# Three hand-written lists of order, written anew, in a retention and soft mixture-of-experts attention kernel

## The chip, the cores and the metric

The kernel runs on one core of a Trainium2 chip. The metric is the device time of one execution in microseconds. Its engines here: TensorE (PE; its weight loads are PEld), VectorE (DVE), ScalarE (ACT), GpSimd (POOL), and SyncE (SP), which issues all loads and stores.

## The reference

Eight sequences of 576 tokens go through causal retention with 8 heads of 64, and then through four attention experts of which a gate takes two for each token.

```python
scores = scale * np.matmul(q, k.transpose(0, 1, 3, 2))     # retention, all heads
Dmat = np.where(rel >= 0, gamma ** rel, 0.0)
x = np.matmul(scores * Dmat, v)                            # then heads side by side: (8, 576, 512)
logits = x @ w_gate                                        # 4 experts, best 2 of them
w = softmax of the two best logits
for e in range(4):
    qe, ke, ve = x @ wq[e], x @ wk[e], x @ wv[e]           # 64 wide
    a = softmax(scale * qe @ ke.T, causal)
    out += (weight of e, where e is among the two) * (a @ ve @ wo[e])
```

## The kernel before, in words

The tokens are cut into 36 tiles of 128, two chunks of 64 each; nine tiles are a pair of sequences. Eight of the nine hold neighbouring chunks of one sequence, the ninth (n % 9 == 8) holds the last chunk of both. Three tiles make a group; there are 12 groups. A group passes three stages, one step apart:

- retention, tile by tile: loads lx and lk (queries and keys, keys and values), dc (decay of the values), qm, qa, qp (scores of the chunk, their copy, the causal cut), tm, tv (state of the chunk, added to the running state), om, oa (product with the state of earlier chunks, "old"), wm, wv (product with the chunk's own scores, added), sc (scaling), xh, xl (split into a rounded part and a rest).
- projections of the group before: vm, va, vv (expert values and gate logits), g.0 to g.4 (the gate; g.1 is an exponent on ScalarE, the others are VectorE), km, ka and hm, ha (expert keys and queries, two halves each).
- attention of the group before that, by units: s (scores), r (their limit, on VectorE, which reads PSUM), e (exponent), n (factor), ma or mv (norm on ScalarE or VectorE), tt (transposes through TensorE), ca or cv (their copies out of PSUM on ScalarE or VectorE), ym (product with the values), ya, yp (copy and split).
- one step later still: pm (output projection, four blocks of 128 columns), pa (copy and store).

A unit is a tile, or one of the two halves of a ninth tile; so every third group has four units and the others three. In a step j the retention tokens with number i mean tile 3j + i, the projections belong to group j - 1, the units to group j - 2 and the outputs to group j - 3; where that group or unit does not exist, the token does nothing. So the first step has no pm, and s.3 exists in steps 4, 7 and 10 only. The second digit of a token such as tt.21 is the chunk of blocks within the unit, of r, e, ma, mv the expert.

The order is written by hand as three strings of such tokens: HEAD (groups 0 and 1 of the pipeline), STEP (played for j = 2 to 11) and TAIL (the drain; `@13` sets j for the tokens that follow). PE, DVE, ACT and POOL run their instructions exactly in the order in which the tokens name them; SP is not among these engines, and its loads and stores are placed by the framework. `:v` puts a decay, scaling or rest on VectorE, which is on POOL otherwise.

```python
ORDERED = {mybir.EngineType.PE, mybir.EngineType.DVE, mybir.EngineType.Activation, mybir.EngineType.Pool}
...
pool = ctx.enter_context(tc.tile_pool(name="ps", bufs=8, space=bass.MemoryType.PSUM))
ctx.enter_context(tc.manual_schedule(engines=ORDERED))
...
play(HEAD)
for j in range(2, NG):
    play(STEP, j)
play(TAIL, NG)
```

TensorE's array is used in three shapes. qk (L197), st (L170), old (L223), own (L243) and the scores ss (L419, and L427 for halves of a ninth tile) run as 64x64 quarters. The projections pj (L316) and pv (L335), the output po (L565) and the transposes pt (L498) use the full array. The values product ys (L532, L536, L539) uses 128x64 halves. All PSUM tiles come from one pool of eight banks: qk, st, old, own take two, a score unit two or four, every other block one.

Before the lists start, the kernel runs small warming matmuls (L117) and issues the loads of tiles 0 to 3, tables and three of the four weights; fw.o fetches the fourth, wh and wl split a weight into its rounded part and rest, tb fills a table.

## Time and profile before

| | us |
|---|---|
| median of 3 runs (lowest, highest) | 445.7 (445.47, 446.39) |
| the profiled execution's own time | 445.0 |
| its span, first to last instruction | 443.1 |
| TensorE busy | 427.4 (96%) |
| VectorE, ScalarE, POOL busy | 302.4, 275.9, 205.3 |
| mean granted TensorE clock | 0.985 |

The profiled execution's time is 1.9 us above its span, and 0.7 us below the median of the runs. Matmuls are pipelined, so a busy TensorE is not one at its peak: the cost of a block is read from its start to the start of the next. A timeline's row gives start, length, engine, line, operation, output and inputs with their shape, and in brackets the idle time ahead and what ended it.

### The profile page before, as it was taken

Reading aid. Unit: us, or ns where it says so; the run is one execution under the profiler, and the core shown is the slowest. Engines: PE = TensorE matmul, PEld = TensorE weight load, DVE = VectorE, ACT = ScalarE, POOL = GpSimd, SP = SyncE. Lnnn points to the kernel's source line nnn. Section 1 sums busy time; section 2 is a strip of 40 time slices with the busy share of each in tenths; the row PEclk is TensorE's granted clock in tenths of the full one; section 3 lists DMA queues with packets and bytes.
Section 4 is the critical chain, followed back from the end, with each engine's and each line's share of the span. In section 5 each row is a group of like instructions: output and inputs, shape, how many; then the busy total and the mean of one; then the engine's idle time right before and its main releaser. Section 6 shows DMA issues by size and latency. Waiting matters only on the chain.

```text
span 443.1 us, 18830 instructions
## 1 busy us (share of the span) xinstructions
PE 427.4 (96%) x7916; PEld 387.3 (87%) x7916; DVE 302.4 (68%) x1095; ACT 275.9 (62%) x818; POOL 205.3 (46%) x260
## 2 busy tenths in 40 slices
PE   8499899999999999999999999999999999999996
PEld 4489789899879999899988999899988999988796
DVE  1656976877787548668787657687688566567761
ACT  2546585673775566665667477476476658457882
POOL 5516664653744555555644375475365174210300
PEclk9779899999999999999999999999999999999999
DMA  7944641261261144243343046054143001001112
GB/s 267 407 174 155 212 168 47 98 231 36 103 220 40 54 176 135 93 154 115 98 152 115 1 144 218 21 170 172 34 155 128 1 4 72 1 2 38 37 72 72
DMA packets 18899, 50.90 MB, mean 115 GB/s; under 512 B 2304, under 2 KB 9088, under 8 KB 18816
## 3 DMA queue, kind: packets, MB, share of 16 engines
q1 hardware_dynamic: 18816, 49.71, 32.3%
q8 instruction: 63, 1.03, 1.0%
q14 instruction: 20, 0.16, 0.1%
HBM read 40.26 MB, written 9.44 MB: 112 GB/s over the span
## 4 chain that ended last, share of the span: by engine, by line
PE 86%; issue 3%; ACT 2%; DVE 2%; POOL 2%; DMA 2%; SPq 1%; DVEq 0%; POOLq 0%; ACTq 0%
PE pj L316 22%; PE pv L335 11%; PE po L565 11%; PE pt L498 8%; PE ss L419 7%; PE ys L532 7%; PE qk L197 4%; PE own L243 3%; PE old L223 3%; PE st L170 3%; PE ys L539 2%; DMA vk<-vkf 2%; PE ss L427 2%; PE ys L536 2%; POOL p L210 1%
## 5 line engine op out<-in xcount | busy, mean ns | idle before, releaser
L456 ACT ACTIVATE p<-p,nm 128x128 f32<-128x128 f32 (+8 forms) x144 | 79.5, 559 | 6.4 <-DVE nm L443 5.2
L280 POOL TENSOR_TENSOR xl<-x,xh 128x512 fp32r<-128x512 f32 x31 | 41.8, 1349 | 76.9 <-ACT xh L275 76.8
L443 DVE CUSTOM_DVE_ANT_0 p<-ss,mask 128x320 f32<-128x320 f32 (+7 forms) x128 | 51.6, 454 | 16.3 <-PE ss L419 16.1
L210 POOL TENSOR_SCALAR_AFFINE_SELECT p<-p 64x512 f32<-64x512 f32 x72 | 48.9, 679 | 25.5 <-ACT p L204 19.8
L555 POOL CAST yh<-y 128x256 fp32r<-128x256 f32 (+1 forms) x36 | 13.7, 380 | 92.0 <-ACT y L543 92.0
L482 DVE TENSOR_SCALAR p<-p,sm 128x64 f32<-128x64 f32 (+8 forms) x116 | 46.2, 448 | 0.9
L511 DVE COPY pth<-pt 128x512 f32<-128x512 f32 (+2 forms) x56 | 32.5, 624 | 20.9 <-PE pt L498 20.4
L498 PE MATMUL pt<-con,p 128*128 128x128 f32 x360 | 44.4, 273 | 0.1
L263 POOL TENSOR_TENSOR x<-x,gi 128x512 f32<-128x512 f32 x28 | 36.6, 1307 | 16.1 <-DVE x L253 12.5
L498 PEld LDWEIGHTS pt<-con,p 128*128 128x128 f32 x360 | 41.1, 141 | 1.4 <-DVE pth L511 0.4
L480 ACT ACTIVATE p<-p,sm 128x512 f32<-128x512 f32 (+7 forms) x60 | 31.3, 547 | 14.9 <-DVE sm L466 14.7
L532 PE MATMUL ys<-pth,vn 128*64 128x128 f32 (+1 forms) x640 | 39.2, 254 | 0.0
L419 PE MATMUL ss<-k,q 64*64 64x512 f32 (+7 forms) x512 | 37.0, 405 | 0.0
L157 POOL TENSOR_TENSOR vk<-vk,con 128x512 f32<-128x512 f32 x32 | 34.4, 1075 | 0.5 <-DMA vk<-vkf 0.4
L570 ACT ACTIVATE ot<-po 128x384 f32<-128x384 f32 x48 | 22.4, 486 | 19.0 <-PE po L565 18.8
L323 ACT ACTIVATE k<-pj 128x384 f32<-128x384 f32 x24 | 11.8, 491 | 33.7 <-PE pj L316 33.5
L204 ACT ACTIVATE p<-qk 128x256 f32<-128x256 f32 x72 | 23.5, 381 | 14.0 <-PE qk L197 13.5
L532 PEld LDWEIGHTS ys<-pth,vn 128*64 128x64 f32 x640 | 29.0, 138 | 1.4 <-issue 0.9
L253 DVE TENSOR_TENSOR x<-x,own 128x256 f32<-128x256 f32 (+1 forms) x72 | 25.4, 385 | 5.5 <-ACT x L232 4.3
L243 PEld LDWEIGHTS own<-p,vk 64*64 64x64 f32 x1152 | 24.7, 141 | 5.1 <-issue 4.5
L232 ACT ACTIVATE x<-old 128x256 f32<-128x256 f32 (+1 forms) x72 | 22.0, 361 | 11.4 <-PE old L223 11.0
L464 DVE TENSOR_SCALAR sm<-sm 128x4 f32<-128x4 f32 (+1 forms) x40 | 14.8, 371 | 19.6 <-ACT p L456 19.0
(95 smaller groups left out, 1088.2 us busy)
## 6 DMA issues: line engine op xcount, KB each, us to landing
x<-xf SPq DMA_DIRECT2D x36, 512.0 KB, 3.9
...
rg<-wraw SPq DMA_DIRECT2D x1, 8.0 KB, 7.2
```

The lines of the kernel that those rows point to most:

```text
L210: gp.affine_select(w, w, pattern=[[0, 8], [1, 64]], base=0, channel_multiplier=-1, compare_op=OP.is_ge, fill=0.0)
L243: mm(ps[r][HALF[u], g, i], vk[HALF[r], s, 0, 2 * g + u], p[HALF[r], g, s, u], start=True, stop=True)
L280: e.tensor_sub(xl, x32, f(xh))
L316: mm(ps, ww[:, kc, p * 128:(p + 1) * 128], xx[:, kc], start=(i == 0), stop=(i == 11))
L335: mm(ps, xx[:, kc, l0:l0 + 128], ww[:, kc], start=(i == 0), stop=(i == 11))
L419: mm(ps[e][HALF[p]], q[p][HALF[z], l0 + 64 * s:l0 + 64 * s + 64], k[p][HALF[z], kb:kb + ws[e]], start=True, stop=True)
L443: v.tensor_tensor_reduce(p32[:, e, :ws[e]], ps[e], mask[:, 576 - ws[e]:], -1.0, BIG, OP.add, OP.min, nm[:, e:e + 1])
L456: act(p32[:, e, :ws[e]], p32[:, e, :ws[e]], AF.Exp, bias=nm[:, b:b + 1], scale=-1.0, accum_out=sm[:, 0, e:e + 1])
L482: v.tensor_scalar(o, i, rs[:, e:e + 1], None, op0=OP.mult)
L498: nc.tensor.transpose(pt[:, z], src, ident)
L532: mm(py[HALF[z], p], VN[n0 + j][:, e * D:(e + 1) * D], src, start=(j == 0), stop=False)
L565: mm(ps, ww[:, p, d * 128:(d + 1) * 128], yy[:, p], start=(i == 0), stop=(i == 5))
```

## The change

All three lists are replaced; nothing else is touched. Every list still names the same work, so each kernel runs the same blocks of TensorE with the same shapes. What differs:

- STEP begins with qm.1 ahead of om.0. pm.3 comes ahead of vm.2 and pm.2 behind wm.2, where both stood between qm.3 and om.2; qm.3 and om.2 are neighbours now. s.3 comes behind pm.2. The transposes between the projections are placed in fewer runs.
- Scalings sc.1 and sc.2 of STEP go from POOL to VectorE. 22 more norms go to ScalarE, and 10 more transposes' copies to VectorE, over the whole kernel.
- At the end of STEP, g.0 and g.1 come ahead of ca.21, ym.3 ahead of ym.2, and lk.6 is the last token.
- HEAD: dc.0 and dc.2 go to POOL, dc.1 and dc.4 to VectorE, sc.3 and xl.3 to POOL; wm.2 comes ahead of vm.0, tm.3 ahead of both k projections, wl.v ahead of tv.1, and the loads fw.o, lx, lk stand in other places.
- TAIL: hm and km, two output blocks and the last score units change places, with the copies and norms that go with them.

```diff
--- before.py
+++ after.py
@@ -44,38 +44,39 @@
 
 
 HEAD = """
-dc.0:v qm.0 qa.0 qp.0 tm.0 tv.0 dc.1 qm.1 qa.1 qp.1 tb.1 om.0 oa.0 wm.0 wv.0 qm.2 sc.0:v tm.1 wh.v xh.0 wm.1 qa.2
-qp.2 dc.2:v tv.1 om.1 oa.1 tm.2 xl.0 wl.v lk.4 wv.1 tb.2 sc.1:v xh.1 xl.1:v tv.2 @1 vm.0 va.0 @0 wh.k om.2 oa.2 wm.2
-@1 vv.0 @0 wv.2 lx.4 @1 vm.1 va.1 @0 sc.2:v qm.3 dc.3 lk.5 qa.3 wl.k qm.4 qp.3 xh.2 xl.2:v @1 vv.1 @0 wh.q fw.o @1
-km.0 ka.0 @0 tm.3 qa.4 @1 km.1 @0 lx.5 @1 ka.1 @0 tv.3 wl.q qp.4 om.3 oa.3 wm.3 lk.6 dc.4 tb.3 wv.3 dc.5 sc.3:v qm.5
-qa.5 qp.5 xh.3 tm.4 @1 hm.1 @0 tv.4 om.4 oa.4 wm.4 xl.3:v tb.4 @1 ha.1 @0 lx.6 tm.5 @1 vm.2 @0 wv.4 dc.6:v tv.5 @1
-va.2 @0 sc.4 @1 vv.2 hm.0 @0 xh.4 @1 g.0 g.1 @0 qm.6 @1 g.2 @0 xl.4:v lk.8 @1 g.3 @0 lx.7 qa.6 om.5 @1 g.4 @0 oa.5
-qp.6 lk.7 wm.5 wv.5 dc.7:v wh.o @1 ha.0 @0 tm.6 tv.6 sc.5 xh.5 wl.o xl.5:v lk.9 lx.8
+qm.0 dc.0 qa.0 tm.0 fw.o tv.0 qm.1 qa.1 qp.0 qp.1 tb.1 om.0 oa.0 wm.0 dc.1:v wv.0 sc.0:v qm.2 wh.v tm.1 wm.1 qa.2
+xh.0 wl.v qp.2 dc.2 tv.1 om.1 tb.2 tm.2 oa.1 xl.0 wv.1 sc.1:v xh.1 xl.1:v wm.2 @1 vm.0 @0 lx.4 @1 va.0 @0 tv.2 om.2
+oa.2 wv.2 dc.3 @1 vv.0 @0 wh.k @1 vm.1 va.1 @0 sc.2:v lk.4 qm.3 qa.3 wl.k qm.4 qp.3 xh.2 tm.3 xl.2:v qa.4 tb.3
+dc.4:v @1 vv.1 @0 tv.3 lx.5 wh.q @1 km.1 km.0 @0 qp.4 wl.q @1 ka.1 @0 om.3 lk.5 oa.3 @1 ka.0 @0 wm.3 wv.3 dc.5 tm.4
+qm.5 lx.6 qa.5 sc.3 xh.3 qp.5 @1 hm.1 @0 wm.4 tv.4 @1 ha.1 @0 lk.6 om.4 lk.8 tb.4 oa.4 xl.3 tm.5 @1 vm.2 @0 dc.6:v
+wv.4 @1 va.2 @0 tv.5 sc.4 @1 vv.2 hm.0 @0 lx.7 xh.4 @1 g.0 g.1 @0 qm.6 xl.4:v @1 g.2 @0 qa.6 @1 g.3 @0 om.5 qp.6
+lk.7 oa.5 @1 g.4 @0 wm.5 wv.5 lk.9 dc.7:v wh.o @1 ha.0 @0 tm.6 tv.6 sc.5 lx.8 wl.o xh.5 xl.5:v
 """
 
 STEP = """
-dc.2 om.0 qm.1 qa.1 qp.1 s.0 r.00 r.01 oa.0 r.02 r.03 wm.0 wv.0 tm.1 tv.1 sc.0 e.00 e.01 e.02 vm.0 va.0 e.03 n.0
-vv.0 ma.02 xh.0 mv.00 xl.0 mv.01 mv.03 lx.3 vm.1 va.1 vv.1 pm.0 pa.0 pm.1 pa.1 qm.2 dc.3 s.1 r.10 lk.4 om.1 qa.2
-oa.1 r.11 tm.2 r.12 e.11 r.13 wm.1 tv.2 qp.2 vm.2 e.10 e.12 lx.4 wv.1 lk.5 e.13 qm.3 n.1 mv.11 pm.3 pa.3 qa.3 pm.2
-e.32 va.2 om.2 oa.2 vv.2 pa.2 sc.1 mv.12 ma.10 xh.1 xl.1 qp.3 s.2 r.21 r.32 r.20 wm.2 wv.2 tm.3 e.21 r.22 r.23 e.20
-tv.3 s.3 km.0 e.22 e.23 sc.2 r.31 mv.33 r.30 r.33 hm.0 n.2 mv.21 tt.03 ka.0 tt.01 mv.32 e.30 mv.20 ma.13 e.31 n.3
-ma.31 dc.4 ma.30 hm.1 tt.00 ma.23 xh.2 mv.22 ca.23 xl.2 cv.00 ha.1 tt.02 lk.6 tt.10 tt.11 km.1 cv.10 cv.03 ha.0 ka.1
-cv.01 lx.5 cv.02 cv.11 tt.12 tt.20 e.33 ca.20 tt.21 tt.30 ca.12 tt.13 cv.13 tt.22 ca.22 tt.32 ca.21 g.0 cv.30 tt.31
-ym.0 ca.32 ya.0 yp.0 ym.1 tt.23 ca.31 g.1 ya.1 cv.33 yp.1 ym.2 ya.2 ym.3 g.2 tt.33 ya.3 yp.2 yp.3 g.3 g.4
+dc.2 qm.1 qa.1 qp.1 om.0 oa.0 s.0 r.00 r.01 wm.0 e.00 r.02 wv.0 tm.1 e.01 lk.4 sc.0 e.02 r.03 vm.0 tv.1 va.0 e.03
+n.0 cv.23 mv.01 ma.02 xh.0 vm.1 mv.00 pm.0 mv.03 pa.0 pm.1 xl.0 vv.0 lx.3 va.1 qm.2 dc.3 vv.1 pa.1 qa.2 s.1 r.10
+om.1 r.11 oa.1 r.12 r.13 tm.2 e.11 qp.2 tv.2 lx.4 wm.1 wv.1 lk.5 pm.3 e.12 vm.2 e.10 pa.3 e.13 n.1 qm.3 qa.3 va.2
+vv.2 sc.1:v om.2 oa.2 xh.1 ma.12 xl.1 s.2 e.32 r.22 ma.10 qp.3 tm.3 r.32 ma.11 r.21 r.20 r.23 wm.2 wv.2 e.21 pm.2
+pa.2 e.20 tv.3 s.3 r.30 r.31 e.23 sc.2:v e.22 hm.0 n.2 e.31 mv.20 ma.13 ma.21 dc.4 ma.32 e.30 n.3 mv.31 km.0 tt.01
+ma.30 mv.22 tt.10 ka.0 tt.00 cv.00 cv.01 mv.23 tt.03 r.33 xh.2 tt.11 cv.10 ca.03 ha.0 lx.5 tt.02 km.1 tt.12 ka.1
+hm.1 ha.1 cv.02 tt.20 cv.12 ma.33 ca.20 tt.32 tt.22 cv.11 tt.30 tt.31 cv.22 xl.2 tt.21 tt.13 ca.32 tt.23 cv.30 ym.0
+g.0 cv.13 g.1 cv.33 ca.21 ya.0 yp.0 ca.31 ym.1 tt.33 ym.3 ya.1 yp.1 ya.3 g.2 yp.3 ym.2 g.3 e.33 ya.2 yp.2 g.4 lk.6
 """
 
 TAIL = """
-s.0 r.00 r.01 r.02 r.03 e.00 e.01 e.02 e.03 n.0 mv.01 ma.02 s.1 r.10 hm.0 ha.0 r.11 e.10 mv.03 r.12 km.1 km.0 ka.0
-e.11 e.12 r.13 e.13 n.1 mv.11 mv.10 ma.13 hm.1 ka.1 ha.1 ma.12 s.2 r.20 r.23 vm.0 r.21 r.22 e.20 tt.11 e.21 e.22
-va.0 vv.0 e.23 ma.00 n.2 mv.20 mv.23 vm.1 va.1 @13 s.0 @12 vv.1 ma.21 ma.22 @13 r.00 @12 vm.2 @13 r.02 r.03 @12 va.2
-vv.2 g.0 g.1 @13 r.01 @12 g.2 ca.11 g.3 pm.0 g.4 pa.0 pm.1 pa.1 tt.10 tt.02 tt.12 tt.00 ca.10 ca.12 tt.21 ca.21
-tt.13 ca.02 @13 e.00 @12 tt.01 tt.03 tt.20 cv.20 ca.01 tt.22 ca.13 ca.00 ca.23 @13 s.1 @12 ca.03 @13 r.10 r.13 @12
-cv.22 @13 r.12 e.01 r.11 e.02 e.03 n.0 mv.01 e.12 ma.02 mv.03 mv.00 @12 pm.2 pa.2 pm.3 pa.3 tt.23 ym.0 ya.0 yp.0 @13
-e.11 @12 ym.2 ya.2 yp.2 @13 tt.00 cv.00 e.10 r.22 tt.01 cv.01 tt.02 cv.02 tt.03 cv.03 e.13 e.32 @12 ym.1 ya.1 yp.1
-@13 n.1 ma.10 ma.22 ma.11 s.3 r.30 s.2 r.20 ma.12 r.21 r.31 r.32 e.20 e.21 r.33 pm.2 pa.2 e.22 e.23 n.2 pm.1 mv.13
-e.30 pa.1 mv.20 mv.21 e.31 ma.23 pm.0 pa.0 tt.11 ma.32 tt.10 e.33 n.3 ma.31 mv.30 pm.3 tt.33 pa.3 tt.13 tt.12 cv.10
-cv.13 tt.20 cv.20 mv.33 tt.21 ca.11 ca.12 ca.21 tt.22 tt.30 ca.30 tt.31 tt.32 cv.33 ca.22 cv.23 cv.32 ca.31 ym.0
-ym.1 yl.1 ym.2 ym.3 yl.0 yl.2 yl.3 @14 pm.0 pa.0 pm.2 @13 tt.23 @14 pm.1 pa.1 pa.2 pm.3 pa.3 @13 r.23
+s.0 r.00 r.01 r.02 r.03 e.00 e.01 e.02 e.03 n.0 mv.02 s.1 r.10 r.11 e.10 hm.0 r.12 ha.0 e.12 e.11 km.0 km.1 ka.0
+r.13 e.13 n.1 s.2 ma.11 tt.11 hm.1 mv.12 ma.13 ka.1 ha.1 r.20 r.21 vm.0 r.22 e.20 mv.01 r.23 e.21 e.22 va.0 vv.0
+e.23 ma.00 mv.10 n.2 mv.20 vm.1 @13 s.0 @12 va.1 mv.23 ma.21 vv.1 @13 r.02 @12 mv.22 ma.03 @13 r.00 @12 vm.2 va.2
+vv.2 @13 r.03 @12 g.0 g.1 @13 r.01 @12 g.2 cv.11 pm.1 tt.10 g.3 pm.0 g.4 pa.0 tt.21 pa.1 ca.10 tt.02 cv.12 tt.00
+ca.02 tt.12 ca.21 tt.01 tt.03 tt.20 tt.13 ca.00 cv.20 ca.01 @13 e.00 @12 tt.23 tt.22 @13 e.02 @12 cv.23 @13 s.1 r.13
+@12 cv.22 @13 r.12 e.01 r.11 r.10 e.03 n.0 @12 pm.2 ca.13 ca.03 @13 e.12 ma.02 @12 pa.2 @13 ma.03 @12 pm.3 @13 mv.01
+@12 ym.0 ya.0 @13 mv.00 @12 yp.0 @13 e.11 @12 ym.2 ya.2 yp.2 @13 tt.00 tt.03 cv.00 e.10 r.22 tt.01 tt.02 cv.01 cv.02
+ca.03 e.13 @12 ym.1 pa.3 @13 e.32 @12 ya.1 yp.1 @13 n.1 ma.10 ma.22 s.2 r.20 ma.12 r.21 s.3 e.22 ma.11 r.31 e.20
+e.21 r.33 r.30 ma.13 pm.2 pa.2 e.23 e.31 r.32 e.30 pm.0 n.2 pm.1 mv.23 tt.11 pa.1 ma.21 tt.10 cv.10 mv.33 e.33 n.3
+mv.20 pa.0 ma.31 tt.13 tt.12 mv.30 pm.3 tt.21 tt.33 mv.32 cv.13 pa.3 cv.11 tt.20 r.23 ca.20 cv.12 tt.22 tt.30 cv.30
+cv.21 tt.31 cv.22 tt.32 cv.23 ca.32 ym.0 ym.1 ca.31 cv.33 yl.1 ym.2 ym.3 yl.0 yl.2 yl.3 @14 pm.0 pa.0 pm.3 pa.3 pm.2
+@13 tt.23 @14 pm.1 pa.1 pa.2
 """
 
 
```

## The prediction

> **What bounds the kernel now.** I read the page first (busy shares, chain that ended last), then the windows by stage, then TensorE's own timeline, where the gap from one block's start to the next's is what that block costs.
>
> ```profile
> PE 427.4 (96%) x7916; PEld 387.3 (87%) x7916; DVE 302.4 (68%) x1095; ACT 275.9 (62%) x818; POOL 205.3 (46%) x260
> ...
> PE 86%; issue 3%; ACT 2%; DVE 2%; POOL 2%; DMA 2%; SPq 1%; DVEq 0%; POOLq 0%; ACTq 0%
> ```
>
> ```profile
> core 0: us, PE busy (x) PEld busy (x) DVE busy (x) ACT busy (x) POOL busy (x), PEclk, DMA share, GB/s
> ...
> 47.70:50.20 2.50, 0.40 (x28) 0.27 (x19) 2.44 (x8) 1.29 (x2) 1.46 (x3) 1.00 0.73 226
> 50.20:57.00 6.80, 6.78 (x152) 6.66 (x152) 5.77 (x20) 3.81 (x15) 5.90 (x5) 0.75 0.68 230
> ...
> 216.60:256.00 39.40, 39.40 (x756) 35.42 (x751) 28.86 (x104) 25.39 (x71) 19.56 (x27) 1.00 0.31 103
> 390.00:443.10 53.10, 49.27 (x537) 43.51 (x535) 29.35 (x124) 36.32 (x104) 3.33 (x6) 1.00 0.13 46
> ```
>
> TensorE carries 86% of the chain, and a middle step has it busy for all of 39.40 us at a granted clock of 1.00. A list can save time there in two ways only: less TensorE time lost at the joints between blocks, or fewer waits that busy time hides. VectorE has 28.86 of 39.40 us (73%) and ScalarE 25.39, so neither is the bound; only the place of an instruction in its queue matters. The head has real holes (0.40 us busy in 2.50 us), and after that one the clock was 0.75 for 6.8 us. Of the last 53.10 us TensorE is busy for 49.27; what is left is mostly the end, where the last copies and stores run.
>
> **The change, part by part.**
>
> *Fewer changes of array mode.* The joints are seen in this stretch of one step:
>
> ```profile
> 187.64 0.63 PE L335 MATMUL pv<-whv,xh 128*128 128x260 f32 x4
> ...
> 189.07 0.51 PE L565 MATMUL po<-yh,who 128*128 128x384 f32 x2
> ...
> 190.13 0.51 PE L565 MATMUL po<-yh,who 128*128 128x384 f32 x2
> ...
> 192.13 0.64 PE L223 MATMUL old<-x,s 64*64 64x64 f32 x32
> 192.59 0.69 PE L170 MATMUL st<-vk 64*64 64x64 f32 x32
> ...
> 193.73 0.75 PE L335 MATMUL pv<-whv,xh 128*128 128x260 f32 x4
> ...
> 195.36 0.69 PE L197 MATMUL qk<-x 64*64 64x64 f32 x32
> 195.98 0.62 PE L565 MATMUL po<-yh,who 128*128 128x384 f32 x2
> ...
> 197.15 0.52 PE L565 MATMUL po<-yh,who 128*128 128x384 f32 x2
> ```
>
> A pv block (12 matmuls) among full-array blocks takes 189.07 - 187.64 = 1.43 us; between two 64x64 blocks it takes 195.36 - 193.73 = 1.63. An output block takes 190.13 - 189.07 = 1.06 inside, and 197.15 - 195.98 = 1.17 just behind a 64x64 block. A 64x64 block of 32 takes 192.59 - 192.13 = 0.46 inside, and qk alone between full-array blocks takes 195.98 - 195.36 = 0.62. The 0.20 of the pv block holds both its edges, of which the one behind a 64x64 block is 0.11 by the output block, so the other is 0.09. One trip from full array to 64x64 and back costs 0.09 + 0.16 + 0.11 = 0.36 us, all of it on TensorE's path.
>
> Written out for each step, with what a step doesn't have left out (outputs of the first step, score units that a group lacks), the old list makes four such trips: qm.1 to tm.1, qm.2 to wm.1, the lone qm.3, and om.2 to tm.3. The new one joins qm.3 to om.2 by putting pm.3 ahead of vm.2 and pm.2 behind wm.2. Only where the group has a fourth unit (steps 4, 7 and 10) does s.3 then stand alone, and the count stays four. The first and the last step have three before and after. So steps 3, 5, 6, 8 and 9 save one trip each: 5 x 0.36 = 1.8 us. Bounds 0 (each joint's cost returns as a wait at the next block) and 2.2; I take 1.8, as the step has no other wait that would be uncovered. The tail keeps its number of trips.
>
> Transposes against projections cost nothing at the joint:
>
> ```profile
> 169.06 6.45 PE pj L316 x36
> ...
> 205.81 2.11 PE pj L316 x12
> ...
> 246.39 2.73 PE pt L498 x25
> ```
>
> A projection between transposes takes 2.11, in a row 6.45/3 = 2.15. Three such trips go in steps 3, 6 and 9 and one comes in the tail: 0 (bounds 0 and 0.2 gained).
>
> *The fourth score unit.* The two tail units have the same shape:
>
> ```profile
> 232.13 1.16 PE L427 MATMUL ss<-k,q 64*64 64x512 f32 x16
> 233.10 0.65 PE L243 MATMUL own<-p,vk 64*64 64x64 f32 x32
> ...
> 234.03 1.67 PE L427 MATMUL ss<-k,q 64*64 64x512 f32 x16
> 235.70 0.62 PE L316 MATMUL pj<-xh,whk 128*128 128x384 f32 x2
> ```
>
> The first takes 0.97 (233.10 - 232.13), the second 235.70 - 234.03 = 1.67. About 0.1 of the difference is its edge, so 0.6 is a wait: the first unit's PSUM banks are still being read by VectorE's limits. Now pm.2, more than 1 us of TensorE work, stands between wm.2 and s.3. It needs one bank where s.3 needs four. I take 0.4 of the 0.6 as gained, in three steps: 1.2 us. Bounds 0 (pm.2 waits instead, since it may be given one of the same banks) and 1.8; it lies nearer the upper end as the work put in between is longer than the wait.
>
> *The head.*
>
> ```profile
> 21.51 0.58 PE L170 MATMUL st<-vk 64*64 64x64 f32 x10 [3.38 <-issue]
> ...
> 30.80 0.98 PE L316 MATMUL pj<-xh,whk 128*128 128x384 f32 x4 [0.80 <-ACT xh L275]
> ...
> 33.11 0.69 PE L170 MATMUL st<-vk 64*64 64x64 f32 x32
> 33.73 0.45 PE L316 MATMUL pj<-xh,whk 128*128 128x384 f32 x1
> ...
> 50.22 0.54 PE L223 MATMUL old<-x,s 64*64 64x64 f32 x16 [2.12 <-DVE s L185]
> 50.58 0.66 PE L197 MATMUL qk<-x 64*64 64x64 f32 x32
> 51.05 0.53 PE L419 MATMUL ss<-k,q 64*64 64x64 f32 x16
> ```
>
> tm.3 stood between km.0 and km.1 for 33.73 - 33.11 = 0.62, while TensorE waited 0.80 for xh.2 just ahead of km.0. It now stands in that hole, and the two projections follow each other: 0.62 and about 0.2 for the joints, 0.8 in sum. At the seam to the first step the second half of om.0 waited 2.12 for tv.6; qm.1 (51.05 - 50.58 = 0.47) now goes ahead and fills part of it: 0.47. This swap of qm.1 and om.0 is worth 0 in all other steps, where om.0 doesn't wait. Head in sum: 1.3.
>
> Against it stand the moves to other engines. dc.0 and dc.2 go to POOL, dc.1 and dc.4 to VectorE, and wl.v goes ahead of tv.1. So tm.2 has to wait for qp.2 and then dc.2, both on POOL:
>
> ```profile
> 16.25 1.36 POOL L210 TENSOR_SCALAR_AFFINE_SELECT p<-p 64x512 f32<-64x512 f32 x2 [3.31 <-DVE vk L157]
> ```
>
> ```profile
> L157 POOL TENSOR_TENSOR vk<-vk,con 128x512 f32<-128x512 f32 x32 | 34.4, 1075 | 0.5 <-DMA vk<-vkf 0.4
> ```
>
> That is 16.25 + 1.36 + 1.08 = 18.7, still ahead of 21.51, where TensorE resumed in tm.2 after 3.38 us of "issue", a wait for nothing that the profile shows. om.1 behind wl.v comes in the same stretch. If that wait stays where it is in TensorE's stream, whose order is the same up to there, both moves cost 0; if it starts later by the delay, an estimate of 1.1 us (qp.2 no longer running beside dc.2). If it ends earlier, the head gains up to 21.51 - 18.7 = 2.8. I take 0, as nothing in the change aims at it. fw.o stands first instead of late, but the queue of loads (SP) isn't one of the four engines that the lists order, so its transfer may move little: 0, the cover being that wh.o is needed only in the last lines of the head. lk.6 at the end of a step has until the dc.3 of the next, several us, and nothing waits for it today.
>
> *The queues in a step.* sc.1 and sc.2 go from POOL to VectorE:
>
> ```profile
> L263 DVE TENSOR_TENSOR x<-x,gi 128x512 f32<-128x512 f32 x4 | 2.9, 725 | 0.5 <-ACT gi L150 0.4
> ```
>
> Twenty of them add 20 x 0.725 = 14.5 us to VectorE, of which some of the norms moved to ScalarE take back most; some turn copies come over. VectorE stays near 75 to 80% of a step: 0 by itself. What can cost is order. ca.21, which ym.2 reads, now stands on ScalarE behind g.1, and g.1 waits for VectorE's g.0, which stands behind cv.22:
>
> ```profile
> 280.44 0.15 DVE L370 TENSOR_REDUCE mx<-lg 128x3 f32<-128x12 f32 x1
> ...
> 280.63 0.16 DVE L372 TENSOR_TENSOR ex<-lg,mx 128x12 f32<-128x12 f32 x1
> ...
> 281.56 1.36 PE L498 MATMUL pt<-con,p 128*128 128x128 f32 x11
> ...
> 284.27 0.61 PE L532 MATMUL ys<-pth,vn 128*64 128x128 f32 x8
> ```
>
> ```profile
> L511 DVE COPY pth<-pt 128x384 f32<-128x384 f32 x22 | 11.9, 550 | 10.6 <-PE pt L498 10.4
> ...
> L509 ACT ACTIVATE pth<-pt 128x512 f32<-128x512 f32 x31 | 17.7, 598 | 1.1 <-PE pt L498 1.1
> L379 ACT ACTIVATE ex<-ex 128x12 f32<-128x12 f32 x12 | 2.6, 214 | 1.5 <-DVE ex L372 1.5
> ```
>
> In steps 2, 5, 8 and 11 ym.2 comes 284.27 - 281.56 = 2.71 us behind the last transposes' start. In the new order seven transposes (0.8) and their latency (0.2), cv.22 (0.55), g.0 to its third instruction (0.35), the exponent (0.21) and ca.21 (0.6) come to 2.7: it just fits. I allow 0.1 us in each of four steps, 0.4. Bounds 0 and, if VectorE comes 0.5 us late to cv.22, 2.0.
>
> The tail's new order I put at 0: same trips, 49.27 us of 53.10 already busy, two score units and two output blocks changing places. Bounds 1 us either way, an estimate: a quarter of the 3.8 us in which TensorE isn't busy there.
>
> *The sum.* 1.8 + 1.2 + 1.3 - 0.4 = 3.9 us, against the profiled execution: span 443.1 to 439.2, time 445.0 to 441.1. The median of the runs shown is 0.7 above that execution, so the forecast for the median is **441.8 us** against 445.7, 0.9% less.
>
> **The rivals.**
>
> *Half the gain.* The joints are saved, but the waits move: pm.2 takes over the wait of s.3 (1.2 lost) and the head gives nothing (1.3 lost). Then 441.8 + 2.5 = 444.3. For it: in the head the same chain through VectorE to tv.6 ends the hole, whatever TensorE does ahead. Against: tm.3 leaves a place where nothing else waited.
>
> *Slower: g.0 ahead of ca.21.* In the four steps above, and through it the whole seam to the next step, ym.2 waits on VectorE's queue. It eats the gain of 3.9 us if ca.21 comes 1.0 us late in each (4 x 1.0), and at 2 us late the time is 441.8 + 8.0 - 0.4 = 449.4. For it: no slack in the sum above, and VectorE gets more to do ahead. Against: VectorE is idle a quarter of a step, and in the other steps a longer ym block or a third one stands ahead of ym.2.
>
> *The clock stays up at the seam.* After the hole at 47.70 to 50.20 the clock was 0.75 for 6.80 us; at full clock the same work takes 5.1. If the shorter hole (1.65 us instead of 2.12) no longer lowers it, 1.7 more are gained: 440.1. For it: the hole gets a fifth shorter. Against: most of it remains.
>
> *Transposes in longer runs.* The first run of transposes in a step grows from 4 or 7 to as many as 19 (about 2.1 us). If the clock fell behind it, the two projections that follow (2 x 2.1) would double: over 40 us in ten steps, near 484. The row of 25 transposes in 2.73 us lies in a stretch with a granted clock of 1.00, so I give it 1 in 100. [...]
>
> *No change in the modes' cost* is not open: 0.62 against 0.46 for the same block is on TensorE's own path.
>
> **How the numbers follow.** Forecast (440.5 to 443.3): 0.50. Clock stays up, or a shorter wait for issue (438.5 to 440.5): 0.14. Half the gain (443.3 to 444.8): 0.13. Within 0.2%, about what a measurement of this kernel can tell from no change (444.8 to 446.6): 0.11, where small waits of queue order eat the rest. Slower, nearly all by ca.21 or by a head that starts 1 to 2 us later: 0.12, of which 0.01 for the transposes. Faster is 0.50 + 0.14 + 0.13 = 0.77, same 0.11, slower 0.12. The range from 439.3 to 445.8 leaves out about 0.05 below and 0.14 above.
>
> **What would show it.** Middle steps: TensorE still busy throughout, no lone qk block, the time from one step's first block to the next's shorter by 0.36 in steps 3, 5, 6, 8, 9. The second tail unit near 1.1 us instead of 1.67, and pm.2 without a wait. Head: no st block between the two k projections, the om wait at the seam about 1.6 us, the clock after it telling the third rival. The forecast is wrong if waits of ys for ScalarE's pth copies (L509) appear, if TensorE's first projection starts later than 22 us, or if pm.2 waits for VectorE's limits.

## The result, and the profile after

The changed kernel is slower. Timed against the kernel before on the same chip, 19 runs of each, its median is 446.94 us against 444.83; the ratio of the times is 1.0067, 95% interval 1.0041 to 1.0093. Each ratio here is of the fast runs, those within 1.5% of the fastest of the same kernel, and is not the quotient of the two medians. Forecast was 441.8, 0.9% faster. The profiled execution of after has a span of 447.5 us (time 449.36, at the upper end of its runs, 445.0 to 451.8), so its trace shows somewhat more loss than the median. Within the runs of after the time goes with the granted clock: the four with a mean clock of 0.977 or less took 449.4 to 451.8 us, the four with 0.991 or more 445.0 to 447.0, and the profiled execution (0.975) is one of the former. The mean of all 19 is 0.985, and that of the kernel before 0.984 to 0.986 in its runs beside the experiments, so the loss as a whole is not a lower clock. Lines of the kernel after are numbered one higher than before (own is L244, the limits' reads L359, the values' copy L350).

The busy shares and the chain of the page after, to set beside those of before:

```profile
PE 428.7 (96%) x7916; PEld 390.5 (87%) x7916; DVE 278.9 (62%) x1086; ACT 283.0 (63%) x845; POOL 184.8 (41%) x242
...
PE 89%; ACT 4%; issue 2%; DMA 2%; DVE 1%; POOL 1%; SPq 0%; ACTq 0%; POOLq 0%; DVEq 0%
```

TensorE does the same 7,916 matmuls and is the chain as before. ScalarE's share of the chain went from 2% to 4%. VectorE was busy for less, not more (302.4 to 278.9 us): 37 norm instructions went to ScalarE (116 to 79 on VectorE), 19 scalings and 10 transposes' copies came, and many of its small instructions took less time each than before.

Windows of after: the stretch behind the seam between head and steps, and the seventh step.

```profile
core 0: us, PE busy (x) PEld busy (x) DVE busy (x) ACT busy (x) POOL busy (x), PEclk, DMA share, GB/s
...
49.40:57.00 7.60, 7.10 (x84) 6.76 (x82) 5.86 (x24) 4.50 (x18) 4.64 (x5) 0.55 0.45 146
219.05:258.80 39.75, 39.60 (x780) 35.86 (x776) 26.84 (x105) 26.19 (x73) 17.20 (x25) 1.00 0.32 102
```

Two columns of PE tell the story: in the middle step it is still busy for 39.60 of 39.75 us, so the loss doesn't show as idle time there; and behind the seam the clock was lower (0.55) than before (0.75). What is lost within a step has to be read from block to block. For that the next table takes, from each timeline, the start of the first own product of a step (wm.0) to that of the next; the last two columns are the sum from step 3 to step 11, and what then remains of the span. The kernels are those told of below; e8_fetch, whose lists are those of before, is left out.

```
step              3      4      5      6      7      8      9     10     sum   rest
before        32.39  38.57  32.37  32.32  38.59  32.11  32.36  38.62  277.33  84.0
after         35.39  38.78  32.50  32.49  38.64  32.04  33.61  38.60  282.05  84.9
e1_head       32.66  38.64  32.32  32.29  38.65  32.11  32.28  38.60  277.55  84.4
e2_step       33.02  39.05  32.57  32.54  38.60  32.10  33.74  38.59  280.21  84.4
e3_tail       32.27  38.57  32.22  32.27  38.59  32.11  32.36  38.63  277.01  84.6
e4_join       32.25  38.27  32.23  31.91  38.21  31.76  31.93  38.27  274.82  84.1
e5_copies     33.80  39.12  32.26  31.93  38.14  31.77  33.02  38.16  278.20  85.1
e6_early      33.23  38.60  32.69  32.49  38.60  32.03  36.05  38.60  282.29  85.2
e7_late       35.05  39.08  32.25  32.49  38.87  32.08  32.49  38.60  280.92  84.8
e12_border    32.57  38.67  33.04  32.49  38.59  32.69  32.49  38.59  279.14  84.6
e11_po        33.33  38.98  32.24  32.51  39.00  32.03  33.33  39.00  280.41  84.6
e9_both       33.06  38.28  31.99  31.97  38.27  31.82  32.91  38.28  276.58  84.6
e10_headjoin  33.20  38.24  31.90  32.92  38.26  31.75  32.00  38.30  276.59  84.4
e13_best      31.95  38.38  32.02  32.99  38.24  32.16  31.97  38.56  276.26  84.1
```

The first row of it starts and ends at these two rows of the timeline of before, the second at the two rows of after that follow them:

```profile
81.73 0.47 PE L243 MATMUL own<-p,vk 64*64 64x64 f32 x20
...
359.06 0.46 PE L243 MATMUL own<-p,vk 64*64 64x64 f32 x18
```

```profile
80.54 0.47 PE L244 MATMUL own<-p,vk 64*64 64x64 f32 x20
...
362.59 0.45 PE L244 MATMUL own<-p,vk 64*64 64x64 f32 x9
```

At step 3 after is 1.2 us ahead (81.73 - 80.54). That alone says little of the head: a run told of below with the old head and the old steps, e3_tail, gets there at 80.42. The eight steps, forecast to save 3.0 by joints and score units, lose 4.7. Most of that stands in steps 3 and 9, and the timeline of TensorE shows where:

```profile
94.05 0.28 PE L244 MATMUL own<-p,vk 64*64 64x64 f32 x4
94.61 0.59 PE L244 MATMUL own<-p,vk 64*64 64x64 f32 x25 [0.28 <-DVE lg L359]
96.30 0.33 PE L244 MATMUL own<-p,vk 64*64 64x64 f32 x3 [1.10 <-issue]
96.56 0.62 PE L566 MATMUL po<-yh,who 128*128 128x384 f32 x2
...
299.81 0.51 PE L566 MATMUL po<-yh,wlo 128*128 128x384 f32 x2
301.16 0.75 PE L336 MATMUL pv<-whv,xh 128*128 128x260 f32 x4 [0.84 <-PE po L566]
```

An own block that takes 0.46 us inside its run takes 96.56 - 94.05 = 2.51 here. It waits twice: 0.28 us for VectorE to read lg, the gate logits in the PSUM bank of pv, and 1.10 us for "issue", in the middle of a block, three matmuls before its end. In step 9 more than a microsecond passes from the start of one block's last row to the next block (299.81 to 301.16), and the view gives TensorE itself as the releaser.

Step 3 lost 3.0 us in this execution, more than these waits. Much of the rest is the clock, which was at half for 3.41 us right behind the wait (a row of the windows, PEclk 0.50):

```profile
97.35:100.76 3.41, 3.41 (x13) 3.41 (x12) 1.63 (x7) 2.20 (x8) 2.63 (x3) 0.50 0.59 211
```

TensorE is busy through all of it, so it costs some 1.7 us, an estimate. In before the clock is 1.00 through its step 3 (81.00 to 113.50 us).

Two suspects came of it.

Theory F: TensorE's own instructions arrive late. Counted in the trace (weight loads, matmuls and the waits for semaphores among them), the one that waits at 96.30 is number 4033 and the one at 301.16 is number 11713; the 3.38 us of issue in the head of before stand at number 705. All are 193 + 256 x n (n = 15, 45, 2). The page of before lists an instruction queue with 63 packets, 1.03 MB, so 16 KB each, and TensorE has some 16,100 instructions so counted, 63 x 256.

Theory C: the copies of the values' product come too late. va.2 and vv.2 stand on ScalarE behind qa.3, the copy of the next tile's scores, in both lists. In the old one vd<-pv is written 4.53 us behind the start of pv (193.73), and nobody minds: pm.3 and pm.2, 2.2 us of work that needs two banks, stand between qm.3 and the next 64x64 blocks. This is the row of ScalarE in before:

```profile
198.26 0.56 ACT L349 ACTIVATE vd<-pv 64x128 f32<-64x128 f32 x2
```

In the new list om.2, s.2, tm.3 and wm.2 follow qm.3 at once and ask for two banks each (s.2 for two or four), one after the other; the pool has eight, and pv still holds one.

### The profile page after: what moved, and what is told of

Its sections match the earlier page's. It is cut to its first block, busy times and chain, and to the rows that moved or that the text cites. A ratio compares the mean times of both kernels' runs of the same rounds, so it can differ in the third digit from the quotient of the medians.

```text
span 447.5 us, 18817 instructions
## 1 busy us (share of the span) xinstructions
PE 428.7 (96%) x7916; PEld 390.5 (87%) x7916; DVE 278.9 (62%) x1086; ACT 283.0 (63%) x845; POOL 184.8 (41%) x242
## 3 DMA queue, kind: packets, MB, share of 16 engines
q8 instruction: 62, 1.02, 1.0%
## 4 chain that ended last, share of the span: by engine, by line
PE 89%; ACT 4%; issue 2%; DMA 2%; DVE 1%; POOL 1%; SPq 0%; ACTq 0%; POOLq 0%; DVEq 0%
PE pj L317 23%; PE pv L336 13%; PE po L566 11%; PE pt L499 8%; PE ss L420 7%; PE ys L533 7%; PE qk L198 4%; PE own L244 4%; PE st L171 4%; PE old L224 3%; PE ys L540 2%; DMA gi<-gi 2%; PE ys L537 2%; PE ss L428 1%; ACT p L481 1%
## 5 line engine op out<-in xcount | busy, mean ns | idle before, releaser
L457 ACT ACTIVATE p<-p,nm 128x64 f32<-128x64 f32 (+7 forms) x144 | 79.4, 556 | 9.6 <-DVE nm L444 6.4
L444 DVE CUSTOM_DVE_ANT_0 p<-ss,mask 128x128 f32<-128x128 f32 (+7 forms) x128 | 51.9, 453 | 33.3 <-PE ss L420 33.2
L512 DVE COPY pth<-pt 128x512 f32<-128x512 f32 (+2 forms) x66 | 38.0, 615 | 26.7 <-PE pt L499 26.2
L481 ACT ACTIVATE p<-p,sm 128x64 f32<-128x64 f32 (+6 forms) x97 | 43.3, 493 | 16.0 <-DVE sm L467 16.0
L171 PE MATMUL st<-vk 64*64 64x64 f32 x1024 | 24.9, 226 | 6.1 <-POOL vk L158 3.0
L276 ACT ACTIVATE xh<-x 128x512 fp32r<-128x512 f32 x36 | 22.5, 625 | 12.3 <-DVE x L264 8.9
L244 PEld LDWEIGHTS own<-p,vk 64*64 64x64 f32 x1152 | 24.8, 139 | 5.4 <-issue 5.2
L171 PEld LDWEIGHTS st<-vk 64*64 64x64 f32 x1024 | 21.7, 140 | 8.8 <-issue 3.5
L244 PE MATMUL own<-p,vk 64*64 64x64 f32 x1152 | 27.6, 225 | 1.6 <-issue 1.3
L465 DVE TENSOR_SCALAR sm<-sm 128x4 f32<-128x4 f32 (+1 forms) x40 | 7.9, 196 | 34.1 <-ACT p L457 34.1
L483 DVE TENSOR_SCALAR p<-p,sm 128x384 f32<-128x384 f32 (+8 forms) x79 | 27.8, 397 | 1.0
```

Of the source, the lines that this page charges most:

```text
L171: mm(ps[r][HALF[g], s, u], vk[HALF[r], s, 1, h], vk[HALF[r], s, 0, h], start=True, stop=True)
L244: mm(ps[r][HALF[u], g, i], vk[HALF[r], s, 0, 2 * g + u], p[HALF[r], g, s, u], start=True, stop=True)
L444: v.tensor_tensor_reduce(p32[:, e, :ws[e]], ps[e], mask[:, 576 - ws[e]:], -1.0, BIG, OP.add, OP.min, nm[:, e:e + 1])
L457: act(p32[:, e, :ws[e]], p32[:, e, :ws[e]], AF.Exp, bias=nm[:, b:b + 1], scale=-1.0, accum_out=sm[:, 0, e:e + 1])
L481: act(o, i, AF.Copy, scale=rs[:, e:e + 1])
```

## The experiments

All ratios below are to the kernel before, run beside it on the same chip, with 95% intervals.

**The three lists one by one.**

```
e1_head:  HEAD  of after, STEP and TAIL of before
e2_step:  STEP  of after, HEAD and TAIL of before
e3_tail:  TAIL  of after, HEAD and STEP of before
```

> The kernel before with the new list of the head alone. The prediction's step: 1.3 us faster (ratio 0.997), and in the trace the first own product of the third step begins about 1.2 us earlier, as it did in the changed kernel (80.54 against 81.73). Rival, that the head's gain is spent again before the steps begin or at the end: within 0.2% of the kernel before. Theory F (TensorE's instructions are fetched in blocks of 256 and a short block runs dry) expects the 3.6 us wait marked issue near 18 us to stay, and no other wait of that kind over 0.5 us, since the steps' list is the old one.

Measured: 443.74 us, 0.9978 (0.9964 to 0.9993): 1.0 us faster. The trace reaches step 3's first own product at 80.34, no evidence by itself beside the 80.42 of e3_tail. Both places of the forecast for the head can be seen in its timeline:

```profile
29.98 0.65 PE L170 MATMUL st<-vk 64*64 64x64 f32 x32
30.96 0.96 PE L316 MATMUL pj<-xh,whk 128*128 128x384 f32 x4 [0.33 <-ACT xh L275]
...
49.31 0.54 PE L223 MATMUL old<-x,s 64*64 64x64 f32 x16 [2.11 <-DVE s L185]
```

tm.3 (st) now stands ahead of the first projection and the wait there is 0.33 instead of 0.80; no st block comes between the projections. The second half of om.0 still waits 2.11 us (2.12 before) although qm.1 went ahead of it: everything at the seam came earlier, and the wait with it.

> The kernel before with the new list of the steps alone. The prediction's steps (joints 1.8, score unit 1.2, queue order -0.4) would make it 2.6 us faster. Theory F (fetch of TensorE's instructions runs dry in the new long runs of 64x64 blocks) expects it slower by 2 to 5 us: waits marked issue of 1 us and more inside the state and own products of at least one step, at those of TensorE's instructions whose number is 193 modulo 256. Theory C (the values' copies now stand behind the score product's copy on ScalarE, so a bank comes free late and own products wait 0.3 to 0.4 us in each step) expects 1.5 to 3 us slower with the loss spread evenly, some 0.3 us in every step, and no issue wait needed.

Measured: 447.86 us, 1.0051 (1.0029 to 1.0073), single runs from 444.8 to 452.3, a wider spread than before has (443.2 to 446.4). So the loss is in the steps' list. The waits of TensorE in this trace hold both suspects:

```profile
PE own L243 <- issue: 0.8, 3, 0.3
...
PE own L243 <- DVE lg L358: 0.6, 2, 0.3
```

Steps 5, 6 and 8, which should save 0.36 each, come out at 32.57, 32.54 and 32.10 against 32.37, 32.32 and 32.11: loss in each step, as theory C has it, and 1.4 us more in step 9, as theory F has it.

> The kernel before with the new list of the tail alone. The prediction: 0 +-1 us. What the two traces show between the last step's own product and the end: 84.0 us before, 84.9 us after, so 0.9 us slower (ratio 1.002) if the loss belongs to the tail's list and not to where the step left the queues.

Measured: 445.11 us, 1.0005 (0.9989 to 1.0021). The time can't tell it from nothing. The traces lean to a small loss: the rest after step 11 has begun is 84.6 to 85.2 us in the eight with the new tail and 84.0 to 84.4 in the six with the old one. The three lists multiply to 1.0034 against 1.0067 for the whole; with these intervals that is no disagreement, nor a proof that they add.

**Is a joint worth 0.36 us at all?**

```diff
-... lk.5 e.13 qm.3 n.1 mv.11 pm.3 pa.3 qa.3 pm.2 e.32 va.2 om.2 oa.2 vv.2 pa.2 sc.1
+... lk.5 e.13 pm.3 pa.3 pm.2 va.2 qm.3 n.1 mv.11 vv.2 pa.2 qa.3 e.32 om.2 oa.2 sc.1
```

> The kernel before, its steps' list changed in one place: the two output projections pm.3 pm.2 stand ahead of the score product qm.3, straight behind the values' product vm.2, and the copies of each follow in that order. This takes away the same number of changes of array mode as the changed kernel does (143 against 159), by joining full-array work and not by lengthening the runs of 64x64 blocks where the loads stand, with the copies in order of their products. If a joint is worth 0.36 us wherever its neighbours do not wait, it is 8 joints, 2.9 us faster. Theory F expects 1 to 2.9 us faster. Theory C as well, since va.2 keeps its place. If it is not faster, a saved change of mode is worth nothing in this kernel, and the row of lone score products from which the 0.36 was read measured something else.

Measured: 443.26 us, 0.9954 (0.9935 to 0.9974): 2.0 us faster. In the table each step is shorter, 2.5 us in eight steps, 0.31 for a joint if each step saves one. The joined stretch of step 6 has no wait in it:

```profile
194.00 0.51 PE L565 MATMUL po<-yh,who 128*128 128x384 f32 x2
...
195.06 0.52 PE L565 MATMUL po<-yh,who 128*128 128x384 f32 x2
...
196.20 0.69 PE L197 MATMUL qk<-x 64*64 64x64 f32 x32
196.72 0.65 PE L223 MATMUL old<-x,s 64*64 64x64 f32 x32
```

The two outputs take 1.06 and 1.14, and qk 0.52. By the order of the matmuls in the traces this edit has 16 changes of array mode less than before, one trip in each of steps 3 to 10; the changed kernel has 12 less, five trips in the steps and one in the head, so the expectation's "same number" does not hold. The price of a joint was near enough right; what went wrong lies in how the changed kernel saves it.

**The values' copies.** One edit of the changed kernel:

```diff
-... e.13 n.1 qm.3 qa.3 va.2 vv.2 sc.1:v om.2
+... e.13 n.1 va.2 qm.3 vv.2 qa.3 sc.1:v om.2
```

> The changed kernel with one edit in its steps' list: the values' copies va.2 and vv.2 stand ahead of, and between, the score product qm.3 and its copy qa.3, in the order in which TensorE ends their products. Theory C: the bank comes free early, the own products wait 0.3 to 0.4 us less in each step that lost them: 1.5 to 3 us faster than the changed kernel, so 444 to 445.5 and a ratio to the kernel before of 0.998 to 1.002. Theory F: the copies are not the cause; within 0.2% of the changed kernel's 1.0067, with the issue waits of 1 us still at instructions 4033 and 11713.

Measured: 445.63 us, 1.0012 (0.9988 to 1.0037), against 1.0067 without the edit. Steps 6, 7, 8 and 10 fall to 31.93, 38.14, 31.77 and 38.16, that is 0.34 to 0.46 us below before: the saving that the prediction had priced, in full. Steps 3, 4 and 9 stay long. How the order does it shows on ScalarE and TensorE in step 6, first after, then this run:

```profile
197.00 0.64 PE L336 MATMUL pv<-whv,xh 128*128 128x260 f32 x4
...
199.03 0.65 PE L224 MATMUL old<-x,s 64*64 64x64 f32 x32
...
199.25 0.66 ACT L205 ACTIVATE p<-qk 128x256 f32<-128x256 f32 x2 [1.18 <-PE qk L198]
...
199.79 0.55 ACT L350 ACTIVATE vd<-pv 64x128 f32<-64x128 f32 x2
...
199.81 0.99 PE L420 MATMUL ss<-k,q 64*64 64x192 f32 x16
```

```profile
194.80 0.65 PE L336 MATMUL pv<-whv,xh 128*128 128x260 f32 x4
...
196.43 0.56 ACT L350 ACTIVATE vd<-pv 64x128 f32<-64x128 f32 x2 [0.56 <-PE pv L336]
...
196.84 0.65 PE L224 MATMUL old<-x,s 64*64 64x64 f32 x32
...
197.05 0.66 ACT L205 ACTIVATE p<-qk 128x256 f32<-128x256 f32 x2
...
197.31 0.94 PE L420 MATMUL ss<-k,q 64*64 64x192 f32 x16
```

In after, ScalarE idles 1.18 us until TensorE has finished qk, while pv, which ended earlier, waits to be copied: vd starts 2.79 us behind the start of pv. With the copy ahead it starts 1.63 behind. The copy of pv comes 1.2 us earlier against its product, and with it the release of its bank and the queues behind (lg on VectorE, x and p on ScalarE). TensorE shows what that is worth: from old to ss 0.47 us (197.31 - 196.84) instead of 0.78 (199.81 - 199.03), and the own block takes 0.62 instead of 0.81.

**The fetch by itself.** The kernel before with 1,280 products of 64x64 behind its end:

```diff
     play(TAIL, NG)
+    pw = [bank([128, 2, 64], "pw") for r in range(2)]
+    for i in range(320):
+        for r in range(2):
+            for g in range(2):
+                mm(pw[r][HALF[g], i % 2], ident[HALF[r], :64], ident[HALF[r], :64], start=True, stop=True)
```

> The kernel before, and behind its last product 1280 more products of 64x64 (2560 TensorE instructions), whose result nobody uses: a measurement by itself. In the kernel 32 such products take 0.46 us, which gives 18.4 us. Theory F: the fetches set the pace, one block of 256 in 3.3 us or more, so 10 blocks take 33 us or more, in bursts of 128 products followed by an issue wait of 1.4 us or more. If TensorE runs them at 0.46 us for 32 without waits, theory F falls.

Measured: the span grew from 443.1 to 512.8 us. Each product is two matmuls and two weight loads, which the expectation had missed, so there were 5,120 instructions, 20 blocks, in 69.7 us: 3.5 us a block. At the pace of the kernel's blocks (32 matmuls in 0.46 us) the work is 37 us. The page's rows for the instruction queue, before and here, then the timeline and the waits of this run:

```profile
q8 instruction: 63, 1.03, 1.0%
```

```profile
q8 instruction: 82, 1.34, 1.1%
```

```profile
460.42 2.09 PE L636 MATMUL pw<-con 64*64 64x64 f32 x128 [1.65 <-issue]
463.89 2.09 PE L636 MATMUL pw<-con 64*64 64x64 f32 x128 [1.38 <-issue]
```

```profile
PE pw L636 <- issue: 29.7, 19, 1.9
```

Bursts of exactly 128 matmuls (256 instructions with their loads), then a wait of 1.4 to 1.9 us, 19 times, with one 16 KB packet for each. "Issue" here is a wait for instructions, and theory F is shown as a mechanism: in this run no block of 256 instructions followed the one before in under 3.47 us. The packets of the queue, read singly, give the parts: the fetch starts 1.1 to 1.5 us after TensorE passes a border, takes 0.9 to 1.4, and TensorE goes on 1.3 to 1.5 after it has landed. Where TensorE is slower (full-array blocks), the fetch can start ahead of the border's own matmul, by up to 46 instructions in this trace; with the 12 to 18 that full-array blocks take in 1.1 us (72 of pj in 6.45 us, 24 of pv in 1.43), the sequencer runs ahead of the array by some 60, an estimate. The 63 packets of 16 KB during the span of before are room for 63 x 256 instructions, about as many as TensorE has, so most of them are moved while the program runs.

**Moving the borders.** Dummy products at the start change nothing but the numbers of the instructions behind them:

```diff
-    warm(40, 16)
+    warm(32, 16)    # e6_early
+    warm(48, 16)    # e7_late
+    warm(80, 16)    # e12_border
```

> The changed kernel with 8 of the 40 short dummy products of its start left out, which are done while TensorE waits for its first load: nothing but the numbers of all later TensorE instructions changes, by 16. Theory F: the borders of the fetched blocks of 256 fall 16 instructions later in the work, the sum over all blocks of what they are shorter than 3.6 us (the shortest time between fetches in the trace) falls from 5.8 to 4.5 us, so 1.3 us faster than the changed kernel (ratio to before 1.003 to 1.004). Theory C and every theory that lies in the order of the work: no difference, 1.0067.

> The changed kernel with 48 short dummy products at its start in place of 40: all later TensorE instructions have numbers that are higher by 16. Theory F: the sum of the blocks' shortfalls rises from 5.8 to 8.4 us, so 2.6 us slower than the changed kernel and 3.9 us slower than with 32 (ratio to before 1.012); the issue wait near 296 us (ninth step) grows to 1.7 us and more, since its block would last 1.9 us. Theory C: no difference from the changed kernel and from the kernel with 32.

Measured: e6 446.92 us, 1.0032 (1.0010 to 1.0053); e7 444.77 us, 0.9998 (0.9975 to 1.0021). The waits move with the borders. In step 9 the two waits of after (0.84 at 301.16, 0.23 at 305.44) became one of 1.86 in e6 (with 3.41 us at half clock behind it, in the 36.05 of its step 9), and none in e7, while step 3's grew in e7. The first row is of e6, the second of e7:

```profile
303.15 0.91 PE L244 MATMUL own<-p,vk 64*64 64x64 f32 x23 [1.86 <-issue]
```

```profile
95.44 0.44 PE L244 MATMUL own<-p,vk 64*64 64x64 f32 x11 [2.31 <-issue]
```

But the order of the two times was forecast the wrong way round. The reckoning had put a border at the time of its matmul and not, as the probe then showed, at the time when the sequencer passes it. That alone doesn't explain it either: the run with 48 was 0.7% faster than the one with 40 although the wait in its step 3 is the larger one. Part of it can be the clock: the mean over its runs is 0.990, 0.988 with 32 and 0.985 with 40. What the shift does to the clock was not tried by itself.

> The changed kernel with 80 short dummy products at its start in place of 40: the numbers of all later TensorE instructions rise by 80, the order of the work is the changed kernel's, and the 1.1 us that they last lies ahead of the 2.9 us wait for the second load. The trace of the probe gave the rule: the next block's fetch starts 1.1 us after TensorE's sequencer (up to some 60 instructions ahead of its products) passes a border, and TensorE goes on 1.4 us after it has landed, so 3.5 us for a block, 4.0 to 4.5 where loads delay the fetch. Theory F, reckoned by that rule with the changed kernel's own trace: the waits sum to 1.3 us at 4.0 (2.3 with 40 products) and to 2.6 at 4.5 (6.5 with 40), so 1 to 4 us faster than the changed kernel, ratio to before 0.998 to 1.004, and in the trace no issue wait at 11713 or 4033. Rival, that the borders' place is worth nothing and the run with 48 differed from that with 32 by chance: 1.0067 again.

Measured: 445.48 us, 0.9989 (0.9962 to 1.0016), against 1.0067 (1.0041 to 1.0093) with 40. The same lists, with other instruction numbers, are 0.8% faster; the intervals don't meet. The reckoned 1 to 4 us hold, but the size is less sure than the intervals say. The ratio leaves out the two longest of the twelve runs (448.44 and 449.21 us); with them the mean is 0.06% above that of the kernel before. And the clock goes along: between runs at 0.991 to 0.992 the gain over after is some 0.7%, between those at 0.985 to 0.988 some 0.2% (estimates from the single runs' times and clocks). The trace, of the longest run, has no issue wait at 4033 or 11713, as expected; one of 1.81 us at number 2241 came up at the seam, with 6.83 us at half clock around its end.

**Less 64x64 work at a stretch, and both edits.**

```diff
-... lk.5 pm.3 e.12 vm.2 e.10 pa.3 e.13 ... wm.2 wv.2 e.21 pm.2 pa.2 e.20
+... lk.5 pm.3 e.12 pm.2 pa.3 vm.2 e.10 pa.2 e.13 ... wm.2 wv.2 e.21 e.20
```

> The changed kernel with one edit in its steps' list: the output projection pm.2 goes back from behind wm.2 to straight behind pm.3, ahead of vm.2 and of the long run of 64x64 blocks; the values' copies stay behind the score product's copy. Theory F (the 256 instructions of a fetched block must last 3.45 us, which the run of 64x64 blocks with 1.43 us of vm.2 alone ahead of it doesn't): 1.06 us more of full-array work lies ahead of the run, so the waits at instructions 4033 and 11713 shrink by about 1 us each, and three steps save a joint (3 x 0.36): 2 to 4 us faster than the changed kernel, ratio to before 0.998 to 1.002. Theory C alone: only the joints, 1.1 us faster than the changed kernel, ratio 1.004, with the own products still losing 0.3 to 0.4 us to the values' copies in each step.

Measured: 447.01 us, 1.0058 (1.0035 to 1.0081): no gain over after that is clear of noise. Theory F's range is missed; theory C's 1.004 lies within the interval. The waits at 4033 and 11713 shrank by 0.5 and 0.3 us only, to 0.58 and 0.56, and s.3 got its old wait back, as this row of step 7 shows against the one of after behind it:

```profile
233.14 1.71 PE L428 MATMUL ss<-k,q 64*64 64x512 f32 x16
```

```profile
236.91 1.20 PE L428 MATMUL ss<-k,q 64*64 64x512 f32 x16
238.04 0.96 PE L317 MATMUL pj<-xh,whq 128*128 128x384 f32 x4
```

> Both edits together: pm.2 back ahead of vm.2, and the values' copies ahead of the score product's copy. If the two causes are separate they add: against the changed kernel the 2.4 us that the copies' edit gave (446.9 to 444.5 by ratio 1.0012) and what pm.2 alone gives, so ratio 0.992 to 0.996, 441.5 to 443. By the step times of the copies' run without its issue waits (31.9 us where no unit is split, against 32.3 before, and 37.8 against 38.6), 4 us in the steps and 1.2 in the head: 440. If the fetches still lose 2 us or more, 443 or above, and the waits marked issue show where.

Measured: 443.11 us, 0.9956 (0.9935 to 0.9977), at the upper end of what was expected. On top of pm.2's place the copies' edit is worth 1.0% (1.0058 to 0.9956), on its own 0.55%. Step 3 still holds an issue wait:

```profile
94.53 0.54 PE L244 MATMUL own<-p,vk 64*64 64x64 f32 x22
95.88 0.39 PE L244 MATMUL own<-p,vk 64*64 64x64 f32 x10 [0.81 <-issue]
```

**The join with the new head.** STEP of e4_join, HEAD of after.

> The kernel before with the new head and with the join of pm.3 and pm.2 behind vm.2 in its old steps' list (two edits that gave 1.0 and 2.0 us alone). If they add: 441.9, ratio 0.993. If the head's gain depends on the new steps' list behind it, 443.

Measured: 442.88 us, 0.9956 (0.9937 to 0.9976): the two edits don't add. TensorE's instructions have the same numbers as in e4_join, yet issue waits of 0.96 and 0.67 us came back at numbers 4033 and 7873 (steps 3 and 6 take 33.20 and 32.92 instead of 32.25 and 31.91). The packets show that the fetches came later: the one that number 4033 waited for started 1.2 us after TensorE had passed the border before it instead of 0.4, the one for 7873 after 3.3 us instead of 1.4, and that one took 1.55 instead of 0.95. The new head shifts the work against the loads; whether the loads delay the fetches was not tried by itself. In the traces of before and after instruction packets beside which the other queues took less than a tenth of the DMA engines' time lasted 0.88 to 1.38 us; the fourteen of more than 1.4 us (up to 2.16) all had a larger share beside them (0.13 to 0.85), but so had many of 0.88 to 0.97 (0.5 to 0.94).

**All of it.** e9_both with 80 dummy products and the old tail:

> The changed kernel with both edits of its steps (pm.2 ahead of vm.2, the values' copies ahead of the score product's copy), 80 short dummy products in place of 40, and the old tail (the four traces with the new tail need 84.6 to 85.1 us from the last step's own product to the end, the five with the old 84.0 to 84.4). With both edits alone the ratio was 0.9956. Theory F expects the issue waits of that run (1.0, 0.7 and 0.2 us) to go but for some 1.3 us: 0.7 to 2 us faster; the tail 0.5: ratio 0.990 to 0.993, 440.5 to 441.7 us. Rival, borders worth nothing: 0.9945.

Measured: 440.31 us, 0.9889 (0.9872 to 0.9906), runs from 439.2 to 442.3: 1.1% faster than the kernel before, faster than either kernel and a little beyond the expected range. Step 3 of it against the rows of e9_both above:

```profile
94.69 0.69 PE L243 MATMUL own<-p,vk 64*64 64x64 f32 x32
```

The own block is whole, 32 matmuls in one row without a wait. Steps 3 and 9 take 31.95 and 31.97; step 6 now holds a wait (32.99), 1.02 us at number 8129, which is a border (the view names ScalarE). The six runs had a mean clock of 0.992, those of before beside them 0.984; at 0.991 to 0.992 three of them average 440.1 us and two of before 444.2, so the gain is not the clock alone.

## Why the prediction was wrong, point by point

- **Joints, 1.8 us.** The size was right: 0.31 to 0.39 us a step where nothing else moved (e4_join, and steps 6 and 8 of e5_copies; its steps 7 and 10, 0.45 and 0.46, save no joint and belong to the score unit below). The step that failed is "as the step has no other wait that would be uncovered". Moving pm.3 and pm.2 away from between qm.3 and om.2 took the cover off va.2 and vv.2, which wait in ScalarE's queue for qa.3. The prediction followed TensorE's blocks and one ScalarE copy, ca.21, and not this queue: it looked at what the moved blocks cost at their edges, not at which late copy they had hidden. Its bound of 0 for the joints ("each joint's cost returns as a wait at the next block") was too kind, since the copies' late place costs 0.55 to 1.0%, 2.4 to 4.5 us.
- **Issue waits, put at 0.** The prediction saw the row of 3.38 us of "issue" in the head and held it for a fixed event of the head. It is at a border too, number 705, the same kind of wait that the new runs of five 64x64 blocks (qm.3 om.2 s.2 tm.3 wm.2, 144 matmuls behind 2.5 us of full-array work, pm.3 and vm.2, where the old list had qm.3 alone, then 2.2 us of outputs, and then the rest) met in steps 3 and 9. It is 0.8% here by e12_border, the clock included, and no term of the sum held it.
- **Fourth score unit, 1.2 us.** s.3 took 238.04 - 236.91 = 1.13 us in after, as forecast, 0.54 less than before. In after the blocks ahead gave it back (steps 7 and 10 at 38.64 and 38.60 against 38.59 and 38.62); with the copies mended 0.45 and 0.46 are left of it, in steps 7 and 10 of e5_copies. The term was right, and hidden by the same queue.
- **Head, 1.3 us.** 1.0 us alone (0.3 to 1.6 by its interval). Most of the 0.8 for tm.3 is there: no st block stands between the two projections, and of the wait ahead of them 0.33 is left where 0.18 was reckoned (0.80 - 0.62). The 0.47 for qm.1 at the seam isn't: alone the om wait stays at 2.11. The traces can't part the head further, since two with the old head differ by 1.3 us at step 3 (81.73 and 80.42).
- **ca.21 behind g.1, -0.4 us, and the slower rival (0.12).** No wait of ys for ScalarE's pth copies is among TensorE's waits of after. The rival had the right sign by a mechanism that didn't occur; the one that did is of its kind, a ScalarE copy queued behind work that ends later, at another place of the step.
- **VectorE near 75 to 80% of a step.** It was busy for 26.84 of 39.75 us in the seventh step, 68%. The term taken from it was 0 and stays so.
- **Tail, 0 +-1.** Within it: 0.2 us by the time, about 0.5 by the traces.
- **The clock stays up (0.14).** It didn't in this execution. In after the seam's single wait of 2.12 us became three, one of them at a border of theory F (number 1985), and the clock of the stretch behind was 0.55 for 7.6 us against 0.75 for 6.8:

```profile
46.99 0.33 PE L224 MATMUL old<-x,s 64*64 64x64 f32 x4 [0.65 <-DVE x L254]
47.76 0.91 PE L224 MATMUL old<-x,s 64*64 64x64 f32 x24 [0.43 <-issue]
...
49.99 1.39 PE L171 MATMUL st<-vk 64*64 64x64 f32 x32 [0.50 <-ACT p L205]
```

  The waits don't settle it. In e11_po, whose seam is that of after, they are 0.65, 0.19, 0.27 and 0.50 us, and the clock stays at 1.00:

```profile
47.00:57.00 10.00, 8.33 (x221) 7.27 (x225) 9.48 (x36) 5.91 (x24) 7.62 (x6) 1.00 0.57 189
```

- **Transposes in longer runs (0.01).** That a run of transposes lowers the clock is shown by no run. In after the clock is 1.00 in the seventh step and from 100.80 to 445.40 us as a whole, with the transposes of steps 4 to 11 in it.

The three effects in ratio: the late copies lose 0.55% (0.2 to 0.9, from e5_copies against after), the borders 0.8% (0.4 to 1.2, from e12_border against after, less if the clock is taken out), and the head gains 0.2%. The copies' edit and pm.2's place do not add (0.55 and 0.1% singly, 1.1% together). e13_best, in which both are mended (with pm.2 moved back and the old tail), has 440.3, below the forecast's 441.8; that the changed lists alone, without the two losses, would have met it was not run.

What stays open is why 16 instructions more gain 0.7%, how much of the borders' effect is the clock and what lowers it, and whether loads delay a fetch.
